# A gelu-gated block after a two-axis transform: in 36 units the minus half of the gate is formed from a copy of the even pass instead of a third matmul pass

## The chip, the cores and the metric

The kernel runs on one core of a Trainium2 chip. The metric is device time in microseconds of one execution. The profile of one execution gives a span (first to last instruction), the busy time of each engine and every instruction's start. The engines are TensorE (PE; its weight loads are PEld), VectorE (DVE), ScalarE (ACT), GpSimd (POOL) and SyncE (SP), which here issues the DMAs.

## The reference

```python
X = np.fft.fft(x, axis=1)          # x: 8 x 3008 x 256
X = np.fft.fft(X, axis=2)
x = X.real.reshape(8 * 3008, 256)
g = x @ w_gate                      # 256 x 1536
val = x @ w_val
out = (gelu(g) * val) @ w_out       # 1536 x 256, exact gelu
```

## The kernel before, in words

The input is real, so rows t and T - t of the transformed sequence have the same even part and opposite odd parts. The kernel therefore computes only 1505 of 3008 rows of each of the 8 batches as two planes in Y (`Y[:, 0, :]` even, `Y[:, 1, :]` odd), and makes both the "plus" row (even + odd) and the "minus" row (even - odd) from them. The second transform is folded into the first-layer weights: WE acts on the even plane, WOP on the odd plane, and WOM is WOP times -2, with zeros in the first partition, so that WOP + WOM, added up in one PSUM bank, is the minus odd part (`gen_w`, L399 to L412). Partition 0 of the odd plane holds another row (the "n" row), whose contribution does not change its sign; a copy of that row, spread over all partitions, lies in `nq`, and `WN` (L413 to L422) holds the n row's weights of the value side, per feature.

**Units.** For each batch the 1505 columns are cut into three chunks (`CH`: 481, 512 and 512 columns, in this order) and each chunk into 12 feature blocks of 128: 36 units per batch, 288 in all. Two units (even, odd) form a pair and share a PSUM tile `ps_v` of two banks, `glp`, `glm`, `ev` and `dv`. Each gate has its own bank `ps_g`, of which there are two. ps_v has two tiles, ps_o and ps_d one bank each.

**One loop.** The order of the work is written out by hand: every engine runs its instructions in program order (`_InOrder`, L19 to L25; that is why nearly all rows have L25). Loop u (L857 to L961) issues
- `val_even(u)`: the WE pass of the value; VectorE forms ev = n row x WN + even part;
- `gate_minus(u-1)`: the WOM pass on top of the bank of unit u-1, then ScalarE's Gelu into `glm`;
- `val_odd(u-1)`: the WOP pass of the value; for an odd unit VectorE then forms h = glp x ps_v for both units and dv = 2 ev - ps_v, the minus value;
- `gate_plus(u)`: WE and WOP passes into a fresh ps_g, Gelu into `glp`;
- `minus(u-1)`: for an odd unit GpSimd multiplies glm and dv of the pair into the mirrored columns of h;
- pieces of the next batch's transform: `a_step` (loops 0 to 11 of a batch, matmuls into ps_d and a ScalarE eviction S), `b_steps` as `fills` between the passes (loops 18 to 34, evictions Y on ScalarE), `fold_x` on GpSimd, DMAs;
- `second(8)`: eight matmuls of the second layer (h x Wo into ps_o, 256 columns), taken from a queue; after 24 of them ScalarE copies ps_o to osb and SP stores it. Sometimes it is 6 instead of 8.

So a gate of an ordinary unit takes three first-layer passes (WE, WOP, WOM), a value two. The last batch has no next batch beside it. Unit numbers below count inside a batch: units 0 to 11 have 481 columns (480 for minus), 12 to 35 have 512.

Of the kernel before, what the change touches and what calls it, by code (L numbers as in the profile page):

```python
# [9 lines left out]
FP32 = mybir.dt.float32  # L10
BF16 = mybir.dt.bfloat16
AF = mybir.ActivationFunctionType
# [15 lines left out]
def _sub(base: bass.AP, free_pattern, free_offset, part_start=0, part_num=None):  # L28
    p_step, p_count = base.ap[0]
    if part_num is None:  # L30
        part_num = p_count - part_start
    pat = [[p_step, part_num]] + [list(x) for x in free_pattern]
    off = base.offset + part_start * p_step + free_offset
    return ap_replace(base, ap=pat, offset=off)
# [3 lines left out]
def kernel(  # L38
# [53 lines left out]
    WOP = const_pool.tile([128, 2, F], BF16)  # L92
    WOM = const_pool.tile([128, 2, F], BF16)
    Wo_sb = const_pool.tile([128, NFC, C], BF16)
    WNb = const_pool.tile([128, NFC], BF16)
    WN = const_pool.tile([128, NFC], FP32)
    NQs = [const_pool.tile([128, YW], BF16, name=f"nq{i}") for i in range(2)]
    HXF = NFC - NCH * 2
    hx = const_pool.tile([128, HXF, 128], BF16)
# [41 lines left out]

    def dv_tile():
        return work.tile([128, 2, 512], FP32, tag="dv", bufs=2, name="dv")

    def osb_tile():
        return work.tile([128, 2, C], FP32, tag="osb", bufs=2, name="osb")
# [266 lines left out]

    def gen_wn():
        ps = ps_d()
        for fc in range(NFC):
            for t in range(NCH):
                pe.matmul(
                    ps[:, fc : fc + 1], _sub(wb[(fc // 4 * 512, 1)], [[1, 128]], t * 512 + fc % 4 * 128),
                    CW[:, t, 1, 0:1], start=(t == 0), stop=(t == NCH - 1))  # L420
        vec.tensor_copy(WNb[:, :], ps[:, :NFC])
        vec.tensor_copy(WN[:, :], WNb[:, :])  # L422

    def gen_tf():
        for i, t in enumerate((TP, TQ, T0P)):
# [142 lines left out]


    units = []  # L570
    for b in range(B):
        for ci in range(len(CH)):
            for fc in range(NFC):
                units.append((b, ci, fc))
    hs, banks, duos = {}, {}, {}

    def kind(u):
        b, ci, fc = units[u]
# [2 lines left out]
    def open_unit(u):  # L581
        b, ci, fc = units[u]
        if fc == 0:
            hs[(b, ci)] = h_tile()
        c0, n = CH[ci]
        if u % 2 == 0:
            duos[u // 2] = dict(pv=ps_v(), glp=glp_tile(), glm=glm_tile(), log=[])
            if kind(u):
                duos[u // 2]["ev"] = ev_tile()
        banks[u] = dict(  # L590
            d=duos[u // 2], k=u % 2, pv=duos[u // 2]["pv"][:, u % 2, :],
            glp=duos[u // 2]["glp"][:, u % 2, :], glm=duos[u // 2]["glm"][:, u % 2, :],
            b=b, fc=fc, c0=c0, n=n, nm=n - n % 32, kd=kind(u), fs=slice(fc * 128, (fc + 1) * 128),
            h=hs[(b, ci)], Y=Ys[b], nq=NQs[b % 2], po=0 if n == 512 else 480,
            mo=512 if n == 512 else 0)

    def layer1(r, ps, W, i, eo, n, start):
        m = pe.matmul(
            ps[:, :n], W[:, i, r["fs"]], r["Y"][:, eo, r["c0"] : r["c0"] + n],
            start=start, stop=True, skip_group_check=not start)  # L600
        if i:
            apart(r["d"]["log"], r["k"], m)

    def val_even(u):
        r = banks[u]
        layer1(r, r["pv"], WE, 1, 0, r["n"], True)
        if r["kd"]:
            nm, fc = r["nm"], r["fc"]
            apart(r["d"]["log"], r["k"], vec.scalar_tensor_tensor(
                r["d"]["ev"][:, r["k"], :nm], r["nq"][:, r["c0"] : r["c0"] + nm],  # L610
                WN[:, fc : fc + 1], r["pv"][:, :nm], op0=ALU.mult, op1=ALU.add))
        else:
            layer1(r, r["pv"], WOP, 1, 1, r["n"], False)

    def gate_minus(u):
        r = banks[u]
        layer1(r, r["pg"], WOM, 0, 1, r["nm"], False)
        act.activation(r["glm"][:, : r["nm"]], r["pg"][:, : r["nm"]], AF.Gelu)

    def gate_plus(u, fill):  # L620
        r = banks[u]
        n = r["n"]
        r["pg"] = ps_g()
        layer1(r, r["pg"], WE, 0, 0, n, True)
        fill()
        layer1(r, r["pg"], WOP, 0, 1, n, False)
        fill()
        act.activation(r["glp"][:, :n], r["pg"][:, :n], AF.Gelu)
# [213 lines left out]
        11 + j: (7 + j,) for j in range(5)}  # L842
    reads_first = {12: 0, 14: 1, 17: 2}

    NU = len(units)
    PER = NU // B

    evens = {27 + 2 * q + h: [(0, q, 4 * h, 4 * h + 4)] for q in range(4) for h in range(2)}
    later = {22: ["n"]}
# [7 lines left out]
    for u in range(NU + 2):  # L857
        b, i = divmod(u, PER)
        fills = []
        tail = None  # L860
        held = False
        if u < NU:
            open_unit(u)
            loads = (0, 14, 19) if b else (8, 12, 18)
            if i in loads and b + 2 < B:
                load_x(b + 2, loads.index(i))
            if b + 1 < B:
                for what in plan[min(b, 1)].get(i, ()):
                    if what == "n":
                        tail = lambda b=b: n_step(b + 1)  # L870
                        continue
                    eo, q, lo, hi = what
                    if lo == 0:
                        held = True
                        st[b + 1]["cur"] = b_steps(b + 1, eo, q)
                    fills += st[b + 1]["cur"][0][lo:hi]
                    if hi == 8:
                        tail = st[b + 1]["cur"][1]

        def fill(most=2):  # L880
            for _ in range(most):
                if fills:
                    fills.pop(0)()

        def second(n):
            for _ in range(n):
                if l2q:
                    l2q.pop(0)()

        if u == 0:  # L890
            r = banks[0]
            r["pg"] = ps_g()
            layer1(r, r["pv"], WE, 1, 0, r["n"], True)
            layer1(r, r["pg"], WE, 0, 0, r["n"], True)
            layer1(r, r["pg"], WOP, 0, 1, r["n"], False)
            layer1(r, r["pv"], WOP, 1, 1, r["n"], False)
            for e in later_evacs:
                e()
            n_first(0)
            act.activation(r["glp"][:, : r["n"]], r["pg"][:, : r["n"]], AF.Gelu)  # L900
            plus(r)
        elif u < NU:
            val_even(u)
            if not held:
                fill()
        if 0 < u <= NU:
            gate_minus(u - 1)
            if not held:
                fill()
        early = 0 < u <= NU and banks[u - 1]["kd"]  # L910
        if early:
            val_odd(u - 1)
        if 0 < u < NU:
            gate_plus(u, fill)
            if banks[u]["kd"] == 0:
                plus(banks[u])
        if 0 < u <= NU and not early:
            val_odd(u - 1)
        while fills:
            fill()  # L920
        if tail:
            tail()
        if 0 < u <= NU:
            minus(u - 1)
        if u < NU:
            if b + 1 < B and i == (19 if b else 21):
                n_turn(b + 1)
            if b + 1 < B and i == 30:
                n_read(b + 1)
        if u < NU:  # L930
            if b == 0:
                for e in extra.get(i, ()):
                    e()
                if i < 12:
                    fold_x(1, i // 4, pool, i % 4 * 2, 2)
            if i % 2 and b + 2 < B:
                j = i - 1
                if b:
                    f, fp = next((j - o, n) for n, o, z in ((0, 4, 18), (1, 18, 28), (2, 28, 36)) if j < z)
                else:  # L940
                    fp, f = divmod(j - 12, 8)
                if 0 <= f < 8 and fp >= 0:
                    fold_x(b + 2, fp, pool, f, 2)
            if b + 1 < B:
                for k in (i,) if b else a_first.get(i, ()):
                    if k < 12:
                        a_step(b + 1, k)
                        if k in (5, 7, 11):
                            j0 = {5: 0, 7: 12, 11: 16}[k]
                            z_write(b + 1, j0, 2 * k + 2 - j0)  # L950
                    if b and k in (8, 10, 13):
                        z_read(b + 1, (8, 10, 13).index(k))
                if b == 0 and i in reads_first:
                    z_read(1, reads_first[i])
        if 0 < u <= NU and u % 12 == 0:
            pb, pi = divmod(u // 12 - 1, 3)
            if CH[pi][0] == 0:
                pool.tensor_copy(hs[(pb, pi)][:, :, 1023:1024], lone)
            l2q += l2_steps(pb, pi)
            few = len(l2q) < 96  # L960
        second((6 if few and u % 12 > 5 else 8) if u <= NU else len(l2q))  # L961


# [28 lines left out]
```

## Time and profile before

| | us |
|---|---|
| median of 3 runs (lowest, highest) | 629.68 (628.66, 629.75) |
| the profiled execution | 628.29 |
| its span | 626.2 |
| PE busy | 604.6 |
| DVE busy | 540.8 |
| ACT busy | 473.5 |
| POOL busy | 450.1 |

The span is cut by program order into the start (weights, tables and the first batch's transform, to about 27 us), the eight batches, and a short end. Starts of loops in the trace: loop 0 of batch 3 at about 246.3 us, of batch 7 at about 540.9. A loop takes 1.89 to 2.2 us. Rows of a group give the engine, the operation, output and inputs, partitions x elements with types, the count, busy us, mean ns of one, and the idle time of the engine just before them with what ended it.

### The profile page before, as it was taken

The page shows a single profiled execution, that of the slowest core. Times are in us where ns is not written, and L with a number is a line of the kernel's source. Part 1 is how long each engine was busy: PE and PEld are TensorE (multiplying, and loading weights), DVE is VectorE, ACT ScalarE, POOL GpSimd, SP SyncE. Part 2 cuts the span into 40 slices and gives each one's busy share as a digit, 9 for nine tenths or more (in the row PEclk, how much of TensorE's full clock was granted, in tenths as well). Part 3 has the DMA queues.
Part 4 walks back from the last instruction along what each step waited for, and adds up shares of the span by engine and source line. Part 5 has one row for each costly group of instructions (what it writes and reads, how often), then busy time and mean ns, then how long its engine had stood idle before and what let it go on. Part 6 is the DMA issues. An engine that isn't in the chain of part 4 may idle for free.

```text
span 626.2 us, 12919 instructions
## 1 busy us (share of the span) xinstructions
PE 604.6 (97%) x4527; PEld 402.4 (64%) x4585; DVE 540.8 (86%) x649; ACT 473.5 (76%) x962; POOL 450.1 (72%) x474
## 2 busy tenths in 40 slices
PE   3799999999999999999999999999999999999997
PEld 2446666666666666666666666666666666666665
DVE  8688988898888989888898898889898899999991
ACT  8688778867787777877788777887778877767762
POOL 9297997768868788677777698687885555556552
PEclk9999999999999999999999999999999999999999
DMA  8997524562337613673246533375223612222123
GB/s 290 367 285 235 157 61 116 171 193 89 76 115 207 198 43 75 187 230 104 53 126 173 188 99 76 103 214 187 67 61 97 191 43 51 60 51 51 38 48 85
DMA packets 65874, 82.36 MB, mean 132 GB/s; under 512 B 8202, under 2 KB 59914, under 8 KB 62994
## 3 DMA queue, kind: packets, MB, share of 16 engines
q1 hardware_dynamic: 64098, 80.62, 43.6%
q0 software_dynamic: 1552, 0.79, 0.9%
q8 instruction: 36, 0.59, 0.4%
q14 instruction: 28, 0.23, 0.1%
q10 hardware_dynamic: 160, 0.13, 0.1%
HBM read 45.05 MB, written 37.25 MB: 131 GB/s over the span
## 4 chain that ended last, share of the span: by engine, by line
PE 90%; ACT 3%; DMA 3%; DVE 2%; issue 1%; SPq 1%; ACTq 0%; DVEq 0%
PE ps_o L25 38%; PE ps_g L25 28%; PE ps_v L25 19%; PE ps_d L25 6%; DMA z<-S 1%; DMA wst<-in_moe_w_gate_dram 1%; ACT S L25 1%; ACT glp L25 1%; ACT G L25 1%; ACT glm L25 1%; DMA Ap<-z 1%; DVE dv L25 0%; DVE h L25 0%; SPq L748 0%; ACT osb L25 0%
## 5 line engine op out<-in xcount | busy, mean ns | idle before, releaser
L25 POOL TENSOR_TENSOR h<-glm,dv 128x1024 bf16<-128x1024 bf16 (+1 forms) x138 | 290.9, 2108 | 152.1 <-DVE dv L25 104.5
L25 PE MATMUL ps_o<-Wo_sb,h 128*128 128x256 bf16 x2136 | 277.7, 272 | 0.2 <-ACT osb L25 0.2
L25 DVE SCALAR_TENSOR_TENSOR ev<-nq,WN,ps_v 128x512 f32<-128x512 bf16 (+1 forms) x276 | 202.6, 734 | 62.5 <-PE ps_v L25 43.8
L25 ACT ACTIVATE glm<-ps_g 128x512 bf16<-128x512 f32 (+1 forms) x288 | 169.4, 588 | 107.8 <-PE ps_g L25 70.9
L25 PEld LDWEIGHTS <-h 128*128 128x128 bf16 x2208 | 210.9, 98 | 53.7 <-issue 0.5
L25 ACT ACTIVATE glp<-ps_g 128x512 bf16<-128x512 f32 (+1 forms) x288 | 170.0, 590 | 9.8 <-PE ps_g L25 0.3
L25 DVE TENSOR_TENSOR h<-glp,ps_v 128x1024 bf16<-128x1024 bf16 (+2 forms) x150 | 172.9, 1153 | 4.8 <-ACT glp L25 2.6
L25 DVE SCALAR_TENSOR_TENSOR dv<-ev,ps_v 128x1024 f32<-128x1024 f32 (+1 forms) x138 | 164.8, 1194 | 0.0
L25 POOL TENSOR_TENSOR xf<-xin 128x254 bf16<-128x254 f32 x168 | 118.3, 727 | 0.4 <-PE ps_v L25 0.4
L25 PE MATMUL ps_g<-Y,WOM 128*128 128x512 bf16 (+1 forms) x288 | 107.7, 374 | 0.3
L25 PE MATMUL ps_v<-Y,WOP 128*128 128x512 bf16 (+1 forms) x288 | 107.7, 374 | 0.0
L25 PE MATMUL ps_v<-Y,WE 128*128 128x512 bf16 (+1 forms) x283 | 106.1, 375 | 0.1
L25 PE MATMUL ps_g<-Y,WOP 128*128 128x512 bf16 (+1 forms) x278 | 103.9, 374 | 1.8
L25 PE MATMUL ps_g<-Y,WE 128*128 128x512 bf16 (+1 forms) x248 | 92.5, 373 | 0.0
L25 PEld LDWEIGHTS <-WOP 128*128 128x128 bf16 x576 | 55.8, 97 | 52.8 <-ACT WOP L25 0.3
L25 PEld LDWEIGHTS <-WE 128*128 128x128 bf16 x576 | 56.0, 97 | 31.1 <-issue 1.0
L25 ACT ACTIVATE osb<-ps_o 128x512 f32<-128x512 f32 x93 | 54.8, 589 | 17.2 <-PE ps_o L25 12.8
L25 PEld LDWEIGHTS <-Ap 128*128 128x128 bf16 (+1 forms) x561 | 40.8, 95 | 33.8 <-DMA Ap<-z 0.3
L25 ACT ACTIVATE S<-ps_d 128x512 bf16<-128x512 f32 x82 | 48.6, 592 | 0.2
L25 PEld LDWEIGHTS <-G 128*128 128x128 bf16 x213 | 21.0, 100 | 31.8 <-ACT G L25 9.0
L25 ACT ACTIVATE Y<-ps_d 128x192 bf16<-128x192 f32 (+4 forms) x142 | 34.0, 339 | 0.5 <-PE ps_d L25 0.5
L25 PEld LDWEIGHTS <-WOM 128*128 128x128 bf16 x300 | 29.2, 97 | 4.9
(127 smaller groups left out, 261.3 us busy)
## 6 DMA issues: line engine op xcount, KB each, us to landing
out_dram<-osb SPq DMA_DIRECT2D x358, 64.0 KB
xin<-in_x_dram SPq DMA_DIRECT2D x16, 1024.0 KB
Ap<-z SPq DMA_DIRECT2D x24, 512.0 KB
xin<-in_x_dram SPq DMA_DIRECT2D x8, 896.0 KB
z<-S SPq DMA_DIRECT2D x7, 768.0 KB
z<-S SPq DMA_DIRECT2D x7, 512.0 KB
z<-S SPq DMA_DIRECT2D x13, 256.0 KB
nq<-nrow SPq DMA_DIRECT2D x8, 376.2 KB
```

The lines of the kernel that those rows point to most:

```text
L25: return lambda *a, **k: self._tc.keep_in_program_order(call(*a, **k))
```

## The change

In 36 units the WOM pass of the gate is left out. These are units 25 and 31 of batch 0, units 1, 5, 11, 25 and 31 of batches 1 to 6, and units 5, 11, 25 and 31 of batch 7. All are odd units of their pairs. In such a unit w
- the gate's WE pass is issued at the end of loop w-1, after four of the eight second-layer matmuls (`gate_even`), and ScalarE copies twice the even part from ps_g into `ge` (fp32);
- in loop w the WOP pass adds the odd part, the plus Gelu reads the bank as before, and VectorE forms go = n row x WN[:, 0] - ps_g (`gate_rest`);
- GpSimd adds ge to go, in place: 2 even + 2 n part - plus = minus gate;
- in loop w+2, after that loop's plus Gelu, ScalarE takes the Gelu of go from SBUF into `glm` (`gate_late`), and then the pair's minus product is issued (in loop w+1 before).

`gen_wn` now also computes the gate's n-row weights, doubled (`WN[:, 0, :]`), with 24 more one-column matmuls and one more small VectorE instruction. ge and go have one buffer each.

```diff
-        for fc in range(NFC):
+        for k in range(2 * NFC):
+            i, fc = divmod(k, NFC)
             for t in range(NCH):
                 pe.matmul(
-                    ps[:, fc : fc + 1], _sub(wb[(fc // 4 * 512, 1)], [[1, 128]], t * 512 + fc % 4 * 128),
+                    ps[:, k : k + 1], _sub(wb[(fc // 4 * 512, i)], [[1, 128]], t * 512 + fc % 4 * 128),
                     CW[:, t, 1, 0:1], start=(t == 0), stop=(t == NCH - 1))
-        vec.tensor_copy(WNb[:, :], ps[:, :NFC])
-        vec.tensor_copy(WN[:, :], WNb[:, :])
+        f = lambda t: _sub(t, [[1, 2 * NFC]], 0)
+        vec.tensor_copy(f(WNb), ps[:, : 2 * NFC])
+        vec.tensor_scalar(WN[:, 0, :], WNb[:, 0, :], 2.0, None, op0=ALU.mult)
+        vec.tensor_copy(WN[:, 1, :], WNb[:, 1, :])
...
+    SPLIT = ((25, 31), (1, 5, 11, 25, 31), (5, 11, 25, 31))
+    def split(u):
+        b, i = divmod(u, PER)
+        return i in SPLIT[0 if b == 0 else 2 if b == B - 1 else 1]
...
     def gate_minus(u):
+        if r["two"]:
+            return
...
+    def gate_even(u):
+        r = banks[u]
+        r["pg"] = ps_g()
+        layer1(r, r["pg"], WE, 0, 0, r["n"], True)
+        if r["two"]:
+            r["ge"], r["go"] = ge_tile(), go_tile()
+            nm = r["nm"]
+            act.activation(r["ge"][:, :nm], r["pg"][:, :nm], AF.Copy, scale=2.0)
+
+    def gate_rest(u):
+        r = banks[u]
+        if r["two"]:
+            nm = r["nm"]
+            vec.scalar_tensor_tensor(
+                r["go"][:, :nm], r["nq"][:, r["c0"] : r["c0"] + nm],
+                WN[:, 0, r["fc"] : r["fc"] + 1], r["pg"][:, :nm], op0=ALU.mult, op1=ALU.subtract)
+            pool.tensor_tensor(r["go"][:, :nm], r["go"][:, :nm], r["ge"][:, :nm], op=ALU.add)
+
+    def gate_late(u):
+        r = banks[u]
+        if r["two"]:
+            nm = r["nm"]
+            act.activation(r["glm"][:, :nm], r["go"][:, :nm], AF.Gelu)
+
     def gate_plus(u, fill):
-        r["pg"] = ps_g()
-        layer1(r, r["pg"], WE, 0, 0, n, True)
+        if not r["two"]:
+            gate_even(u)
         fill()
...
             gate_plus(u, fill)
+            gate_rest(u)
...
         if 0 < u <= NU:
-            minus(u - 1)
+            if not banks[u - 1]["two"]:
+                minus(u - 1)
+        if 1 < u and banks.get(u - 2, {}).get("two"):
+            gate_late(u - 2)
+            minus(u - 2)
...
-        second((6 if few and u % 12 > 5 else 8) if u <= NU else len(l2q))
+        if u + 1 < NU and split(u + 1):
+            open_unit(u + 1)
+            second(4)
+            gate_even(u + 1)
+        second((6 if few and u % 12 > 5 else 8) - 4 * (u + 1 < NU and split(u + 1)) if u <= NU else len(l2q))
```

More of the change, by code (lines that the diff above doesn't have):

```diff
@@ L94 @@
     Wo_sb = const_pool.tile([128, NFC, C], BF16)
-    WNb = const_pool.tile([128, NFC], BF16)
-    WN = const_pool.tile([128, NFC], FP32)
+    WNb = const_pool.tile([128, 2, NFC], BF16)
+    WN = const_pool.tile([128, 2, NFC], FP32)
     NQs = [const_pool.tile([128, YW], BF16, name=f"nq{i}") for i in range(2)]
@@ L143, in dv_tile, with ge_tile, go_tile @@
         return work.tile([128, 2, 512], FP32, tag="dv", bufs=2, name="dv")
+    def ge_tile():
+        return work.tile([128, 512], FP32, tag="ge", bufs=1, name="ge")
+    def go_tile():
+        return work.tile([128, 512], FP32, tag="go", bufs=1, name="go")
     def osb_tile():
@@ L570 @@
     units = []
+    NU = B * len(CH) * NFC
+    PER = NU // B
+    SPLIT = ((25, 31), (1, 5, 11, 25, 31), (5, 11, 25, 31))
     for b in range(B):
@@ L593, in open_unit @@
             b=b, fc=fc, c0=c0, n=n, nm=n - n % 32, kd=kind(u), fs=slice(fc * 128, (fc + 1) * 128),
-            h=hs[(b, ci)], Y=Ys[b], nq=NQs[b % 2], po=0 if n == 512 else 480,
+            two=split(u), h=hs[(b, ci)], Y=Ys[b], nq=NQs[b % 2], po=0 if n == 512 else 480,
             mo=512 if n == 512 else 0)
@@ L610, in val_even @@
                 r["d"]["ev"][:, r["k"], :nm], r["nq"][:, r["c0"] : r["c0"] + nm],
-                WN[:, fc : fc + 1], r["pv"][:, :nm], op0=ALU.mult, op1=ALU.add))
+                WN[:, 1, fc : fc + 1], r["pv"][:, :nm], op0=ALU.mult, op1=ALU.add))
         else:
@@ L616, in gate_minus @@
         r = banks[u]
-        layer1(r, r["pg"], WOM, 0, 1, r["nm"], False)
-        act.activation(r["glm"][:, : r["nm"]], r["pg"][:, : r["nm"]], AF.Gelu)
+        nm = r["nm"]
+        if r["two"]:
+            return
+        layer1(r, r["pg"], WOM, 0, 1, nm, False)
+        act.activation(r["glm"][:, :nm], r["pg"][:, :nm], AF.Gelu)
+    def gate_even(u):
[17 more added lines that the diff above has]
+        if r["two"]:
+            nm = r["nm"]
+            act.activation(r["glm"][:, :nm], r["go"][:, :nm], AF.Gelu)
     def gate_plus(u, fill):
@@ L843 @@
     reads_first = {12: 0, 14: 1, 17: 2}
-    NU = len(units)
-    PER = NU // B
     evens = {27 + 2 * q + h: [(0, q, 4 * h, 4 * h + 4)] for q in range(4) for h in range(2)}
@@ L862 @@
         if u < NU:
-            open_unit(u)
+            if not split(u):
+                open_unit(u)
             loads = (0, 14, 19) if b else (8, 12, 18)
```

## The prediction, made before the changed kernel had run

> **What bounds the kernel now.** I read the totals first, then the chain that ended last, the groups by form, the list of waits, and last the timeline round the units that change.
>
> ```profile
> span 626.2 us, 12919 instructions
> ...
> PE 604.6 (97%) x4527; PEld 402.4 (64%) x4585; DVE 540.8 (86%) x649; ACT 473.5 (76%) x962; POOL 450.1 (72%) x474
> ...
> PE 90%; ACT 3%; DMA 3%; DVE 2%; issue 1%; SPq 1%; ACTq 0%; DVEq 0%
> ```
>
> TensorE is busy for 97% of the span and carries 90% of the chain. A busy matmul row alone would prove little, because matmuls overlap (0.38 us each), so I looked at starts. From about 75 us on, a 512-column pass starts 0.216 us before the next matmul, a 480- or 481-column pass 0.203, a second-layer pass (256 columns) 0.109, without gaps. TensorE's issue is the bound: a removed pass shortens the end by its pitch, unless another engine then makes TensorE wait. That is the whole question, since VectorE (86%) is nearly as full.
>
> ```profile
> L25 POOL TENSOR_TENSOR h<-glm,dv 128x1024 bf16<-128x1024 bf16 x96 | 205.9, 2145 | 94.3 <-DVE dv L25 88.4 <-ACT glm L25 3.9 <-ACT glp L25 2.0
> L25 DVE SCALAR_TENSOR_TENSOR ev<-nq,WN,ps_v 128x512 f32<-128x512 bf16 x192 | 142.9, 745 | 37.2 <-PE ps_v L25 18.5 <-PE ps_d L25 18.3
> L25 POOL TENSOR_TENSOR xf<-xin 128x254 bf16<-128x254 f32 x168 | 118.3, 727 | 0.4 <-PE ps_v L25 0.4
> ...
> L25 DVE SCALAR_TENSOR_TENSOR ev<-nq,WN,ps_v 128x480 f32<-128x480 bf16 x84 | 59.7, 711 | 25.3 <-PE ps_v L25 25.3
> ...
> L25 ACT ACTIVATE osb<-ps_o 128x512 f32<-128x512 f32 x89 | 53.2, 598 | 16.4 <-PE ps_o L25 12.4 <-issue 2.5 <-DMA out_dram<-osb 0.6
> ```
>
> These rows (columns: busy us, mean ns | idle before) price the new instructions: ge has the shape of osb, go that of ev, and the GpSimd add lies between xf and h.
>
> **What is removed.** 36 WOM passes: 20 in units 1, 5, 11 (480 columns) and 16 in units 25, 31 (512): 20 x 0.203 + 16 x 0.216 = 7.5 us. The even pass of such a unit w only moves, from loop w to the end of loop w-1; the second-layer passes around it stay as many (4 and 4). The old minus Gelu (0.57 to 0.60) goes from loop w+1 and comes back, reading SBUF, in loop w+2.
>
> **What is added on TensorE.** gen_wn computes 24 columns instead of 12, so 24 more one-column matmuls. The 24 of before start at 42.68 and the next matmul at 43.28: 0.6 us. TensorE is nearly gapless there, so I charge 0.6; the lower end is 0, if it hides in the wait of 0.18 us behind WNb and in the waits for Gelu nearby. The extra WN instruction on VectorE (0.41 like its neighbour) is inside that.
>
> **ge on ScalarE and the WOP pass that waits for it.** ge must read the bank before WOP(w) adds to it. Loops 30 and 31 of batch 3:
>
> ```profile
> 309.77 0.60 ACT L25 ACTIVATE glp<-ps_g 128x512 bf16<-128x512 f32 x1
> ...
> 310.26 0.56 ACT L25 ACTIVATE Y<-ps_d 128x184 bf16<-128x184 f32 x2
> ...
> 310.60 1.22 DVE L25 SCALAR_TENSOR_TENSOR dv<-ev,ps_v 128x1024 f32<-128x1024 f32 x1
> ...
> 311.09 0.38 PE L25 MATMUL ps_g<-Y,WE 128*128 128x512 bf16 x1
> ...
> 311.13 0.60 ACT L25 ACTIVATE glm<-ps_g 128x512 bf16<-128x512 f32 x1 [0.31 <-PE ps_g L25]
> ...
> 311.36 0.38 PE L25 MATMUL ps_g<-Y,WOP 128*128 128x512 bf16 x1
> ...
> 311.73 0.74 DVE L25 SCALAR_TENSOR_TENSOR ev<-nq,WN,ps_v 128x512 f32<-128x512 bf16 x1
> ```
>
> ScalarE can start the next instruction 0.45 us after such a Y pair (302.02 to 302.47 in loop 26). The moved WE(31) starts at about 310.01, its data are readable 0.41 later (WOP 311.36 to glp 311.77 shows that lag), so ge runs 310.71 to 311.30. Loop 31 begins 0.216 later than before but has lost its WE, so WOP(31) still falls due at 311.36. A dependent start follows an end by 0.05 us at least (the smallest distance between ev's end and the WOP pass that waits for it). So ge is just in time. In units 1, 5, 11 an S eviction stands before ge: S at 256.46, ge 256.95 to 257.54, WOP(5) due at 257.69: 0.1 to spare. In batch 7 there is neither S nor Y, and ge is early. ge's own price lies between 0.57 (glm at 480) and 0.714 us (the G row, a read from SBUF with a scale column): a stall of 0 to 0.1 us in each of the 30 units of batches 1 to 6. I take the near row, osb, and 0.05 for the 12 units with Y, none for the rest: 0.6 us. Behind ge stand glm(w-1) and glp(w); ScalarE idles 0.31 to 0.50 before glm there and loses a whole Gelu in loop w+1, so the rest of ge is hidden. If that cover were gone, every 0.1 us of lateness would cost 0.1 us per unit.
>
> **go on VectorE.** go reads the bank that glp(w) reads too. The list of waits of before shows what happens when two engines read one bank:
>
> ```profile
> DVE WOM L25 <- ACT WOP L25: 0.9, 1, 0.9
> ```
>
> There VectorE waited for ScalarE although both only read ps_o, and the instruction order of the changed kernel gives go such a wait on ScalarE. [...]
>
> Where does go hurt? VectorE's queue behind it holds ev(w+1), h, dv, ev(w+2), and TensorE's value pass WOP of unit w+2 waits for ev(w+2). Unit 31, batch 3: glp(31) ends at about 312.42, go starts 312.45, and holds VectorE 0.67 (starts of ev and then h are 0.67 apart: 308.80, 309.47); ev(32), before at 312.91, comes at 313.12: 0.21 late. TensorE is 0.216 earlier from here on. The WOP pass of unit 33 started 0.56 after ev(33) ended: 0.56 - 0.21 - 0.216 = 0.13, above the 0.05 needed: no stall. Units 1, 5, 11: 0.72 us of room against 0.63 + 0.03: no lateness worth naming. By the next pair VectorE has caught up (0.44 and 0.75 us idle per pair).
>
> **Batch 7 is different**: no first transform lies beside it, a pair takes TensorE only 3.90 us instead of 4.1, and VectorE idles 0.24 per pair.
>
> ```profile
> 599.21 0.75 DVE L25 SCALAR_TENSOR_TENSOR ev<-nq,WN,ps_v 128x512 f32<-128x512 bf16 x1 [0.24 <-PE ps_v L25]
> ...
> 602.14 0.74 DVE L25 SCALAR_TENSOR_TENSOR ev<-nq,WN,ps_v 128x512 f32<-128x512 bf16 x1
> 603.12 0.75 DVE L25 SCALAR_TENSOR_TENSOR ev<-nq,WN,ps_v 128x512 f32<-128x512 bf16 x1 [0.23 <-PE ps_v L25]
> ```
>
> ev(31) ends its slot at 602.81; go holds to 603.48, so ev(32) is 0.36 late; the waiting pass had 0.25 to spare: 0.25 - 0.36 - 0.216 = -0.33, with the 0.05 a stall of 0.38, more than the 0.216 gained. The same for unit 25; by the same count 0.18 for unit 5 and 0.12 for unit 11: 1.06 us together.
>
> **The add on GpSimd and the late Gelu.** From xf (254 columns, 727 ns) and h (1024, 2145 ns) a line gives 1.2 us for 512; the ends are 0.73 and 2.15. It is queued behind the minus product of the pair before: 314.06 to 315.26 for unit 31. ScalarE reaches the late Gelu after glp(33), about 316.1, and would hold evictions and the next glm behind it if it waited; 0.8 us to spare, and the high end of 2.15 would just still do. GpSimd's queue then has fold and minus product 0.7 us later, which it makes up in one or two pairs; h is read by the second layer only after its chunk, dv is wanted two pairs later. Cost: nothing. No DMA is added or moved; SP's queue is untouched.
>
> **Sum**: -7.5 + 0.6 + 0.6 + 1.06 = -5.3 us. The profiled execution took 628.29 us (span 626.2 and 2.1 around it), which becomes 623.0. It lies 1.4 below the median of the three runs, 629.68, so I put the forecast on the median: **624.4 us**.
>
> **Rivals.**
> 1. Everything is covered: ge never stalls, batch 7 absorbs go. Only gen_wn is paid: 629.7 - 6.9 = 622.8. For it: TensorE shows hardly a wait. Against: VectorE's idle 0.24 in batch 7. Chance 0.23.
> 2. go is dearer than ev's pitch, because it starts on a wait of its own (0.745 and 0.1 to 0.2 more instead of 0.67): in the 12 units 25 and 31 of batches 1 to 6 the 0.13 to spare turns into a stall of about 0.15, 1.8 us: 626.2. Chance 0.17.
> 3. Slower: the WOP pass waits for ge. ScalarE is in order, and ge ends within 0.1 us of when it is wanted. If ge starts one instruction late (an osb or a longer S in front, 0.45), each of 30 units stalls by 0.4: 12 us, less the 5.9 of a sum without my 0.6: 635.8. It decides from 5.9 / 30 = 0.20 us of wait per unit. Against it: S, Y and glp already stand in the counted times, and osb falls at the end of loops 2, 5, 8 and 11 of a chunk, never just before ge. Chance 0.10.
> 4. Smaller waits of 2 and 3 together cancel the gain: about 629. Chance 0.05.
>
> The forecast keeps 0.45. A measurement of this kernel tells about 0.2% (1.26 us) from no change. Faster by more: 0.23 + 0.17 + 0.45, less a little for 2's upper end = 0.84; within: 0.06; slower: 0.10. The range 621.8 to 628.5 takes in rivals 1 and 2 and the bounds of ge (0 to 3 us), gen_wn and the 1.4 us between profile and median; it leaves out rivals 3 and 4.
>
> **What would show it.** Right: 36 fewer ps_g matmuls with WOM, TensorE still about 97% busy, waits of PE on ge below 0.1 us each, VectorE's busy time up by about 26 us, GpSimd's by about 43 with the add near 1.2 us, and loops 7, 13, 27, 33 of batch 7 with a wait on ev. Wrong: a long total "ps_g <- ACT ge" (rival 3), "glm <- POOL go" on ScalarE, or waits of PE on ev in batches 1 to 6 (rival 2).

## The result, and the profile after

| | before | after |
|---|---|---|
| median, us (lowest, highest) | 629.71 (628.66, 630.04), 4 runs | 623.98 (622.88, 624.58), 4 runs |
| the profiled execution | 628.29 | 624.03 |
| its span | 626.2 | 622.0 |

After / before is 0.991, with a 95% interval of 0.9892 to 0.9928: faster by 0.9%, and inside the forecast's range (624.4; 621.8 to 628.5). The medians differ by 5.7 us, the two profiled executions by only 4.3. Executions of one kernel differ in their first 30 us; the last section shows part of the reason. So the comparisons below count from loop 0 of batch 0 on.

The totals and the chain's shares, on the page of after:

```profile
span 622.0 us, 12960 instructions
...
PE 598.5 (96%) x4515; PEld 399.8 (64%) x4573; DVE 566.0 (91%) x686; ACT 485.1 (78%) x998; POOL 491.4 (79%) x510
...
PE 80%; DVE 6%; DMA 5%; ACT 5%; SPq 2%; issue 2%; ACTq 0%; DVEq 0%
```

VectorE gained 25.2 us of work, GpSimd 41.3, ScalarE 11.6, and TensorE lost 6.1 of busy time; still the span is shorter. TensorE carries the chain as before, with less of it. The new rows, among the groups by form of after (busy us, mean ns | idle before):

```profile
L25 POOL TENSOR_TENSOR h<-glm,dv 128x1024 bf16<-128x1024 bf16 x96 | 206.0, 2146 | 71.8 <-DVE dv L25 50.9 <-ACT glm L25 16.9 <-DVE ev L25 1.5
...
L25 POOL TENSOR_TENSOR go<-go,ge 128x512 f32<-128x512 f32 x16 | 20.4, 1272 | 0.0
...
L25 DVE SCALAR_TENSOR_TENSOR go<-nq,WN,ps_g 128x512 f32<-128x512 bf16 x16 | 11.9, 746 | 0.1
...
L25 ACT ACTIVATE ge<-ps_g 128x512 f32<-128x512 f32 x16 | 9.6, 602 | 0.1
```

The prices were read well: ge 0.602 (osb: 0.598), go 0.746 (ev: 0.745), the GpSimd add 1.27 (1.20 at 480 columns; 1.2 forecast). GpSimd's idle time before the minus product falls (94.3 to 71.8). In the list of waits of after, TensorE's matmuls wait for GpSimd once, 9.0 us for an xf, as in before.

**Where the time went.** I took the start of every unit's value WOP pass in both traces and subtracted, after minus before:

| at | us |
|---|---|
| loop 0 | -0.24 |
| unit 11 of batch 0 | +2.11 |
| end of batch 0 | +1.69 |
| end of batches 1, 2, 3 | +0.68, -0.34, -1.36 |
| end of batches 4, 5, 6 | -2.39, -3.40, -4.42 |
| end of batch 7 | -4.21 |

Three things are in it. First, the kernel after *loses* 2.35 us between units 6 and 11 of batch 0, where it splits nothing. Then it gains 0.42 in batch 0 and 1.02 in each of batches 1 to 6, against removed passes worth 2 x 0.216 = 0.43 and 3 x 0.203 + 2 x 0.216 = 1.04: nearly all of it arrives. In batch 7 it gives 0.2 back.

Why the passes pay in full: unit 25 of batch 3, in the timeline of after.

```profile
296.96 0.58 ACT L25 ACTIVATE Y<-ps_d 128x184 bf16<-128x184 f32 x2
...
297.42 0.60 ACT L25 ACTIVATE ge<-ps_g 128x512 f32<-128x512 f32 x1
...
298.07 0.38 PE L25 MATMUL ps_g<-Y,WOP 128*128 128x512 bf16 x1
...
298.55 0.59 ACT L25 ACTIVATE glp<-ps_g 128x512 bf16<-128x512 f32 x1
...
299.17 0.75 DVE L25 SCALAR_TENSOR_TENSOR go<-nq,WN,ps_g 128x512 f32<-128x512 bf16 x1
```

ge ends at 298.02 and the WOP pass that adds to its bank starts 0.05 later, the smallest distance at which a value WOP pass follows its ev in either trace. It is just in time, as the prediction said. glp ends at 299.14 and go starts 0.03 later.

Batch 7, VectorE's rows of after and then TensorE's, round unit 33:

```profile
600.93 1.22 DVE L25 SCALAR_TENSOR_TENSOR dv<-ev,ps_v 128x1024 f32<-128x1024 f32 x1
602.06 1.40 DVE L25 SCALAR_TENSOR_TENSOR ev<-nq,WN,ps_v 128x512 f32<-128x512 bf16 x2
```

```profile
602.41 0.38 PE L25 MATMUL ps_g<-Y,WOM 128*128 128x512 bf16 x1
602.86 0.38 PE L25 MATMUL ps_v<-Y,WOP 128*128 128x512 bf16 x1
```

VectorE has no gap (dv, then both ev back to back), and the WOP pass follows the WOM pass by 0.45 instead of 0.216: it waits for ev, 0.23 us. Two passes earlier, the value's WE pass (602.20) starts 0.05 after dv ends (602.15), 0.11 late. By the same count of starts the four units cost 0.18 (unit 5), 0.24 (11), 0.33 (25) and 0.34 (31).

The loss of 2.35 us lies in `gen_wn` of batch 0. Timeline of after, VectorE, GpSimd and the pass that comes late:

```profile
44.59 1.57 DVE L25 TENSOR_SCALAR WN<-WNb 128x12 f32<-128x12 bf16 x1
...
44.74 1.39 POOL L25 TENSOR_TENSOR xf<-xin 128x254 bf16<-128x254 f32 x2
46.08 1.58 DVE L25 CAST WN<-WNb 128x12 f32<-128x12 bf16 x1
...
46.23 1.39 POOL L25 TENSOR_TENSOR xf<-xin 128x254 bf16<-128x254 f32 x2
...
48.27 0.36 PE L25 MATMUL ps_v<-Y,WOM 128*128 128x480 bf16 x1 [1.79 <-DVE h L25]
```

Two VectorE instructions of 12 columns take 1.57 and 1.58 us. The first ends at 46.16, 0.03 after GpSimd's two folds at 44.74 to 46.13; the second at 47.66, 0.04 after the next two (46.23 to 47.62). (In the first chunk of batch 0 the kernel works otherwise than in the loop described above: VectorE forms h for each unit by itself, and the value too gets its minus half by a WOM pass, onto the bank that h reads.) The unit's plus product h stands behind the two on VectorE, and TensorE's WOM pass waits 1.79 us for it. In before, the one WN instruction ended at 45.23, 0.03 after two folds (43.79 to 45.20) too:

```profile
43.79 1.41 POOL L25 TENSOR_TENSOR xf<-xin 128x254 bf16<-128x254 f32 x2
...
44.82 0.41 DVE L25 CAST WN<-WNb 128x12 f32<-128x12 bf16 x1
```

Its row, from the groups of before, is what I had taken for its price:

```profile
L25 DVE CAST WN<-WNb 128x12 f32<-128x12 bf16 x1 | 0.4, 411 | 0.0
```

### The profile page after: what moved, and what is told of

The parts are those of the page before. It is cut to its first block, busy times and chain, and to the rows that moved or that the text cites. A ratio compares the mean times of both kernels' runs of the same rounds, so it can differ in the third digit from the quotient of the medians.

```text
span 622.0 us, 12960 instructions
## 1 busy us (share of the span) xinstructions
PE 598.5 (96%) x4515; PEld 399.8 (64%) x4573; DVE 566.0 (91%) x686; ACT 485.1 (78%) x998; POOL 491.4 (79%) x510
## 4 chain that ended last, share of the span: by engine, by line
PE 80%; DVE 6%; DMA 5%; ACT 5%; SPq 2%; issue 2%; ACTq 0%; DVEq 0%
PE ps_o L25 34%; PE ps_g L25 24%; PE ps_v L25 17%; PE ps_d L25 5%; DMA Ap<-z 4%; SPq L791 2%; ACT osb L25 1%; ACT S L25 1%; DVE h L25 1%; DVE dv L25 1%; DVE xf L25 1%; DVE ev L25 1%; DMA wst<-in_moe_w_val_dram 1%; ACT glp L25 1%; ACT glm L25 1%
## 5 line engine op out<-in xcount | busy, mean ns | idle before, releaser
L25 POOL TENSOR_TENSOR h<-glm,dv 128x1024 bf16<-128x1024 bf16 (+1 forms) x138 | 291.2, 2110 | 105.2 <-DVE dv L25 62.7
L25 PE MATMUL ps_o<-Wo_sb,h 128*128 128x256 bf16 x2136 | 283.6, 273 | 1.3 <-ACT osb L25 0.3
L25 PEld LDWEIGHTS <-h 128*128 128x128 bf16 x2208 | 210.9, 98 | 57.3 <-issue 0.5
L25 DVE SCALAR_TENSOR_TENSOR ev<-nq,WN,ps_v 128x512 f32<-128x512 bf16 (+1 forms) x276 | 202.0, 733 | 30.7 <-PE ps_v L25 23.0
L25 ACT ACTIVATE glp<-ps_g 128x512 bf16<-128x512 f32 (+1 forms) x288 | 169.8, 589 | 37.8 <-PE ps_v L25 17.6
L25 ACT ACTIVATE glm<-ps_g 128x512 bf16<-128x512 f32 (+1 forms) x252 | 148.6, 590 | 63.8 <-PE ps_g L25 43.8
L25 DVE TENSOR_TENSOR h<-glp,ps_v 128x1024 bf16<-128x1024 bf16 (+2 forms) x150 | 172.9, 1153 | 5.0 <-ACT glp L25 2.4
L25 DVE SCALAR_TENSOR_TENSOR dv<-ev,ps_v 128x1024 f32<-128x1024 f32 (+1 forms) x138 | 164.8, 1194 | 0.0
L25 POOL TENSOR_TENSOR xf<-xin 128x254 bf16<-128x254 f32 x168 | 118.2, 725 | 0.4 <-PE ps_v L25 0.4
L25 PE MATMUL ps_v<-Y,WOP 128*128 128x512 bf16 (+1 forms) x288 | 107.8, 374 | 0.2
L25 PE MATMUL ps_v<-Y,WE 128*128 128x512 bf16 (+1 forms) x283 | 106.2, 375 | 0.1
L25 PE MATMUL ps_g<-Y,WE 128*128 128x512 bf16 (+1 forms) x267 | 99.8, 374 | 0.0
L25 PE MATMUL ps_g<-Y,WOP 128*128 128x512 bf16 (+1 forms) x259 | 96.8, 374 | 0.7
L25 PE MATMUL ps_g<-Y,WOM 128*128 128x512 bf16 (+1 forms) x252 | 94.5, 375 | 0.3
L25 PEld LDWEIGHTS <-WOP 128*128 128x128 bf16 x576 | 55.8, 97 | 50.7 <-issue 0.6
L25 PEld LDWEIGHTS <-WE 128*128 128x128 bf16 x576 | 56.0, 97 | 28.5 <-issue 2.0
L25 ACT ACTIVATE osb<-ps_o 128x512 f32<-128x512 f32 x93 | 54.8, 589 | 15.7 <-PE ps_o L25 12.5
L25 PEld LDWEIGHTS <-Ap 128*128 128x128 bf16 (+1 forms) x561 | 39.8, 96 | 32.0
L25 ACT ACTIVATE S<-ps_d 128x512 bf16<-128x512 f32 x82 | 48.8, 596 | 1.9 <-PE ps_d L25 1.9
L25 POOL TENSOR_TENSOR go<-go,ge 128x480 f32<-128x480 f32 (+1 forms) x36 | 44.4, 1235 | 0.0
L25 PEld LDWEIGHTS <-G 128*128 128x128 bf16 x213 | 21.1, 100 | 33.5 <-ACT G L25 8.9
L25 ACT ACTIVATE Y<-ps_d 128x192 bf16<-128x192 f32 (+4 forms) x142 | 34.0, 340 | 0.5 <-PE ps_d L25 0.5
```

The lines of the kernel that those rows point to most:

```text
L25: return lambda *a, **k: self._tc.keep_in_program_order(call(*a, **k))
```

## The experiments

Theory A: the gain is TensorE's pitch per removed pass; the loss at WN is a VectorE instruction held while GpSimd's folds run; the loss of batch 7 is go on a full VectorE. The rivals: WN's time is its own or comes from something else; go costs as much in the other batches; ScalarE, where ge is just in time, or GpSimd is the next limit. Kernels with "one run" in their line ran once; what is said of them comes from that execution's trace. The kernel before took 628.62 us (median) beside the first four, 628.73 beside the next three, and 629.64 beside the last three.

| kernel | us (lowest, highest) | to before, 95% |
|---|---|---|
| wn_only | 629.34 (628.48, 631.17) | 1.0014 (1.0002, 1.0026) |
| wn_scalar | 623.39 (622.53, 624.47) | 0.9912 (0.9892, 0.9932) |
| wn_psum | 623.15, one run | |
| b7_plain | 622.83, one run | |
| ge_twice | 640.82, one run | |
| more3 | 623.57 (623.10, 624.25) | 0.9914 (0.9898, 0.9931) |
| more_all | 624.73 (624.32, 625.61) | 0.9937 (0.9922, 0.9952) |
| after_again | 624.66 (623.44, 624.82) | 0.9917 (0.9902, 0.9931) |
| best_a | 623.43 (622.47, 623.82) | 0.9899 (0.9884, 0.9914) |
| best_b | 621.52 (621.02, 622.16) | 0.9868 (0.9852, 0.9885) |

### What the WN weights cost alone: wn_only

```diff
-    SPLIT = ((25, 31), (1, 5, 11, 25, 31), (5, 11, 25, 31))
+    SPLIT = ((), (), ())
```

> The larger gen_wn alone; no unit is split. Theory: the two small WN instructions of VectorE (12 columns, SBUF to SBUF) are held until GpSimd ends its running fold, 1.57 and 1.58 us in the trace of after, and TensorE stands behind them; the span grows by about 2.3 us over before (626.2 to 628.5). Rival, my prediction's term: only the 24 more matmuls count, +0.6 us (626.8).

The first WN took 0.37 us and the second 1.58 (VectorE and GpSimd in the timeline of wn_only):

```profile
44.56 0.37 DVE L25 TENSOR_SCALAR WN<-WNb 128x12 f32<-128x12 bf16 x1
...
44.85 1.58 DVE L25 CAST WN<-WNb 128x12 f32<-128x12 bf16 x1
...
44.99 1.41 POOL L25 TENSOR_TENSOR xf<-xin 128x254 bf16<-128x254 f32 x2
```

The second again ends 0.03 after the folds (46.43 and 46.40). From loop 0 to unit 11 the kernel loses 1.16 us, neither the 2.3 of after nor the rival's 0.6. So the size that I gave for it missed: the wait depends on where in a pair of folds the instruction falls, and that shifts between executions. With the two instructions, after loses 2.35 us there (they take 1.57 and 1.58), after_again, the same kernel, 1.76 (0.97 and 1.58), wn_only and b7_plain 1.16 and 1.17 (0.37 and 1.58), and ge_twice, below, only 0.33 (0.91 and 0.16; the second falls between two pairs of folds).

### The two WN instructions elsewhere: wn_scalar, wn_psum

```diff
-        vec.tensor_scalar(WN[:, 0, :], WNb[:, 0, :], 2.0, None, op0=ALU.mult)
-        vec.tensor_copy(WN[:, 1, :], WNb[:, 1, :])
+        act.activation(WN[:, 0, :], WNb[:, 0, :], AF.Copy, scale=2.0)
+        act.activation(WN[:, 1, :], WNb[:, 1, :], AF.Copy)
```

> After, with both WN instructions on ScalarE. Theory: ScalarE shares nothing with GpSimd, so each takes about 0.2 us and TensorE's wait of 1.79 us in loop 8 of batch 0 goes: span about 1.8 us under after (622.0 to 620.2), 24 more matmuls remain. Rival: the wait belongs to the small instructions as such, whatever the engine, or to the matmuls: no change over 0.4 us.

The instructions of tile WN in wn_scalar (ns: lowest, median, highest), and the folds beside them:

```profile
L25 ACT ACTIVATE WN<-WNb x2: 195/204/212, 45.9 to 46.0; 128x12 f32<-128x12 bf16 x2
```

```profile
45.25 1.41 POOL L25 TENSOR_TENSOR xf<-xin 128x254 bf16<-128x254 f32 x2
```

On ScalarE each takes 0.20 us beside the same folds, and the loss falls from 2.35 to 0.66. In its trace theory A is right. The late Gelu of after, which ScalarE takes from SBUF to SBUF, says the same: 0.62 us for 512 columns beside folds (at 157.64) and with GpSimd idle (at 590.06). That ScalarE shares nothing with GpSimd is shown no further than by these times. The span, 621.5, is not the 620.2 expected: loop 0 starts 1.05 us later than in before (last section). The medians show hardly any of it: 0.9912 to before here, 0.991 for after. Both this loss and the start vary between executions of after, so its median need not hold the 2.35 of its profiled one.

wn_psum leaves the instructions on VectorE and lets them read PSUM:

```diff
-        vec.tensor_copy(f(WNb), ps[:, : 2 * NFC])
-        vec.tensor_scalar(WN[:, 0, :], WNb[:, 0, :], 2.0, None, op0=ALU.mult)
-        vec.tensor_copy(WN[:, 1, :], WNb[:, 1, :])
+        vec.tensor_scalar(WN[:, 0, :], ps[:, :NFC], 2.0, None, op0=ALU.mult)
+        vec.tensor_copy(WN[:, 1, :], ps[:, NFC : 2 * NFC])
```

> After, with WN formed by VectorE straight from PSUM in fp32; the rounding to bf16 in between is left out, so WN differs in its last bits. Theory: with a PSUM source VectorE does not need what GpSimd holds, both instructions take about 0.17 us like the WNb row, and the 1.79 us wait goes. Rival: VectorE is slow on 12-column outputs as such: they stay above 1 us.

Same engine, same size, same neighbours; the source differs, in memory and in type (PSUM, fp32, instead of SBUF, bf16). VectorE and GpSimd in the timeline of wn_psum:

```profile
44.17 1.40 POOL L25 TENSOR_TENSOR xf<-xin 128x254 bf16<-128x254 f32 x2
...
44.94 0.16 DVE L25 TENSOR_SCALAR WN<-ps_d 128x12 f32<-128x12 f32 x1
45.02 0.16 DVE L25 COPY WN<-ps_d 128x12 f32<-128x12 f32 x1
```

Both run in the middle of the folds and take 0.16 us. What remains of the loss is 0.31 us, with the 24 more matmuls. So it is neither the engine nor the size: a copy from this source in SBUF is what waits. No run parts the memory from the type; bf16 in SBUF alone is not slow, for in ge_twice the second WN instruction, between two pairs of folds, takes 0.16. Beside the folds the two took 0.37 to 1.58 us each on VectorE from SBUF, 0.16 on VectorE from PSUM and 0.20 on ScalarE. Why VectorE is held, no run shows.

### Batch 7 without the split: b7_plain

```diff
-    SPLIT = ((25, 31), (1, 5, 11, 25, 31), (5, 11, 25, 31))
+    SPLIT = ((25, 31), (1, 5, 11, 25, 31), ())
```

> After without the four split units of batch 7. Theory: these four cost stalls of 0.18, 0.16 (with 0.08), 0.33 and 0.33 us against 0.2 us each of removed passes, so undoing them takes 0.2 us off the way from the start of batch 7 to the last value pass. Rival: each split is worth its pass here too: undoing them costs 0.84 us.

Against before, b7_plain goes from -5.45 (end of batch 6) to -5.52 at the end; after goes from -4.42 to -4.21. Four splits, which remove 2 x 0.203 + 2 x 0.216 = 0.84 us of passes, cost 0.28 net: 1.12 us of stalls. The rival, by which they gain 0.84, falls.

### ge doubled: ge_twice

```diff
             act.activation(r["ge"][:, :nm], r["pg"][:, :nm], AF.Copy, scale=2.0)
+            act.activation(r["ge"][:, :nm], r["pg"][:, :nm], AF.Copy, scale=2.0)
```

> After with the even copy ge issued twice in a row, so that WOP(w) waits 0.49 us longer for ScalarE. Theory: units 25 and 31 have nothing to spare (WOP starts 0.05 us after ge ends, the least there is), units 1, 5, 11 have 0.13, 0.08 and 0.13, batch 7 0.22: stalls of about 0.49, 0.36, 0.41, 0.36, in all 13 to 14 us over after, span 635 to 636. Rival: ScalarE is idle for 22% of the span and takes it for nothing: under 2 us.

This asks whether ScalarE's idle share (22% in after) covers a late ge. Timeline of ge_twice, unit 25 of batch 3:

```profile
316.55 1.24 ACT L25 ACTIVATE ge<-ps_g 128x512 f32<-128x512 f32 x2
...
317.83 0.38 PE L25 MATMUL ps_g<-Y,WOP 128*128 128x512 bf16 x1 [0.48 <-ACT ge L25]
```

It doesn't. The five units of a batch stall by 0.47, 0.52, 0.47, 0.64 and 0.64 us; the second ge, which writes the same tile, starts 0.60 to 0.64 after the first. The span is 16.7 above after's, more than the 13 to 14 that I expected, because I had spaced the two by 0.49. The rival (idle time takes it in) falls, and the prediction's third rival is real as a mechanism: a ge one instruction late costs every unit its lateness.

### More units: more3, more_all

Both have WN on ScalarE, no split in batch 7, and two buffers for ge and go.

```diff
+    # more3
+    SPLIT = ((25, 31), (1, 3, 5, 11, 25, 31), ())
+    # more_all
+    SPLIT = ((25, 31), (1, 3, 5, 7, 9, 11, 25, 31), ())
```

> WN on ScalarE, no split in batch 7, unit 3 of batches 1 to 6 split as well, two buffers each for ge and go. Theory: a pair of 481 columns has room on VectorE (0.72 us against go's 0.66) and on GpSimd (no fold in loops 1 and 3), so each of the 6 new splits gains 0.2 us: span 1.2 + 1.8 + 0.2 = 3.2 us under after, about 618.8. Rival: VectorE or ScalarE, full in two pairs in a row, give it back: not under 620.0.

> As more3, with units 7 and 9 split too: every pair of the 481-column chunk of batches 1 to 6. Theory A: only TensorE and VectorE count: another 2.4 us, span 616.4. Theory B: GpSimd does not keep up (2.02 + 1.6 + 1.2 = 4.8 us of work against a pair of 4.0 in loops 4 to 11), the late Gelu waits at the head of ScalarE's queue for the add and TensorE stalls: above more3, 619 to 622.

A batch of more3 gains 0.85 us, one of after 1.02: the sixth split loses 0.17 net, although it removes 0.20. ScalarE's rows of more3, in batch 2:

```profile
181.59 0.65 ACT L25 ACTIVATE glm<-go 128x480 bf16<-128x480 f32 x1
182.09 0.65 ACT L25 ACTIVATE S<-ps_d 128x512 bf16<-128x512 f32 x1
```

The late Gelu of unit 1 stands before S. S ends at 182.74, the next a_step matmul into ps_d starts 182.78, 0.16 late. Two loops on, osb is late in the same way, behind the late Gelu of unit 3 and an S, and the second layer waits 0.22 for ps_o:

```profile
185.60 0.61 ACT L25 ACTIVATE glm<-go 128x480 bf16<-128x480 f32 x1
186.09 0.60 ACT L25 ACTIVATE S<-ps_d 128x512 bf16<-128x512 f32 x1
186.57 0.61 ACT L25 ACTIVATE osb<-ps_o 128x512 f32<-128x512 f32 x1
```

Together 0.38, more than the pass is worth. The theory (0.2 more per new split, span 618.8) falls; the span is 622.2, and the rival, by which an engine gives the gain back, stands. more_all gains 0.59 per batch, with another 0.20 (ps_d) and 0.46 (ps_o) of stalls per batch. These stalls too end with an eviction of ScalarE that stands behind a late Gelu. Its span is 623.6, so theory A (616.4) falls. Theory B was right that more splits lose, but not on where: in no split unit of more_all does the late Gelu wait for the add, it starts 0.59 us or more after the add's end. So ScalarE's order is the limit that comes next; GpSimd, the other candidate, is not what TensorE waits for.

### The better version: after_again, best_a, best_b

after_again is the kernel after, unchanged, beside the other two.

> The changed kernel again, beside the two below on one chip. Theory: 0.7 to 0.9% under before; in batch 0 the two WN instructions of VectorE take anything from 0.5 to 3.2 us together, by where GpSimd's folds stand when they start, so this kernel's times spread by some 1.5 us. Rival: they take 3.2 us always.

best_a has WN from PSUM (as wn_psum) and no split in batch 7. Its WN weights, like those of wn_psum and best_b, are not rounded to bf16.

> WN from PSUM and no split in batch 7. Theory: against after the wait behind WN goes (0.9 to 2.0 us) and 0.2 us of batch 7's stalls net: 1.0 to 2.2 us under after_again, ratio to before about 0.988. Rival: the medians of after hold little of the WN wait: under 0.5 us of difference.

best_b adds to best_a unit 3 of batches 1 to 6 and two buffers for ge and go, and moves the late Gelu behind the a_step, that of unit 3 by one more loop:

```diff
-        if 1 < u and banks.get(u - 2, {}).get("two"):
-            gate_late(u - 2)
-            minus(u - 2)
...
+        for v in (u - 3, u - 2):
+            if banks.get(v, {}).get("two") and u - v == (3 if v % PER == 3 else 2):
+                gate_late(v)
+                minus(v)
```

> best_a with unit 3 of batches 1 to 6 split too, the late Gelu issued after the S eviction, and that of unit 3 a loop later, where ScalarE has one Gelu less. Theory: in more3 the new splits gained nothing because S (and through ps_d a transform matmul, 0.16 us) and osb (and through ps_o the second layer, 0.22 us) came late behind the late Gelu; with that order mended the six splits are worth 0.2 us each: 1.2 us under best_a. Rival: the chunk's ScalarE work is too much in any order: not better than best_a.

after_again lies 0.83% under before, as expected; its two WN instructions take 2.55 us together, so the rival (always 3.2) falls. Its 624.66 falls to 623.43 in best_a: 0.31 instead of 1.76 us at gen_wn, and no loss in batch 7 (1.2 us, inside the 1.0 to 2.2 expected). best_b takes 621.52, 1.9 less again. ScalarE's rows of best_b at the place shown above for more3:

```profile
181.09 0.66 ACT L25 ACTIVATE S<-ps_d 128x512 bf16<-128x512 f32 x1
181.57 0.66 ACT L25 ACTIVATE glm<-go 128x480 bf16<-128x480 f32 x1
```

Now S goes first, ps_d is free in time, and a batch gains 1.22 us with six splits (best_a: 1.02 with five): the sixth pays its whole pitch, 0.20, in all batches but one, which has a stall of 0.2. From unit 11 of batch 0 to the end best_b gains 7.40 us on before, best_a 6.50. So the traces show 0.9 of the 1.9 us between their medians (1.2 expected); where the rest comes from is not shown. best_b's ratio to the kernel before, 0.9868 with 0.9852 to 0.9885, is the best here.

## Why the prediction was right

- **TensorE's issue is the bound, 0.216 and 0.203 us per pass**: right. 32 splits in batches 0 to 6 gave 6.53 of 6.68 us.
- **gen_wn, 0.6**: wrong, and the term that missed: 2.35 in the profiled execution, 0.33 to 1.76 in others. The sentence "the extra WN instruction (0.41 like its neighbour) is inside that" failed. The row of 0.41 was not an instruction's work but its wait for a fold; two of them can wait for two pairs of folds. In wn_psum, where the instructions don't wait, 0.31 is left. The matmuls alone were sized well: in after they push the next value pass 0.60 back, and the value pass behind it only 0.25, since the idle time behind WNb, 0.18 in before, is gone.
- **ge's stall, 0.6**: too high. All stalls of batches 0 to 6 together are 6.68 - 6.53 = 0.15. That S, Y and ge are just in time was right; ge_twice shows that nothing lies behind it as cover.
- **go waits for glp**: the start is 0.03 after glp's end nearly everywhere, as the order written into the instructions demands. The wait of 0.9 us in before that stood for it was on ps_d, not ps_o: WOP ends at 25.79 and WOM starts at 25.83. What happens when both engines read the bank at once wasn't tried.
- **go in batches 1 to 6**: right. The WOP pass of unit 33 of batch 3 starts 0.14 after ev's end (0.13 forecast), and unit 27's 0.16. The second rival, 0.15 of stall in 12 units, isn't seen. The first, by which batch 7 absorbs go, falls with the next point.
- **Batch 7, 1.06 of stalls**: right, 1.12 (0.18, 0.12, 0.38 and 0.38 forecast for its units; 0.18, 0.24, 0.33 and 0.34 measured).
- **The add and the late Gelu, nothing**: right. In batches 0 to 6 the late Gelu starts 0.59 to 1.23 after the add's end, in batch 7 0.23 to 0.69, so it never waited. The list of waits of after does name one sign of being wrong, `ACT glm L25 <- POOL go L25: 3.8, 5, 0.8`; but these five are ordinary Gelus from ps_g, whose own WOM pass started less than 0.5 us before. What the steps missed lies ahead of it on the same engine: the late Gelu delays S and osb. At five units per batch that costs nothing; at six it does (more3).
- **The sum**: -7.5 + 2.35 + 0.15 + 1.12 = -3.9 from loop 0 on; with the 0.24 that the profiled after was ahead by then and 0.07 that batch 7 gains in b7_plain too, -4.2, as the spans say (-5.3 forecast). That the median lies only 0.4 from the forecast is luck: the sum was too good by 1.1 (gen_wn 1.75 dearer, ge 0.45 cheaper, 0.31 from before loop 0 and from the end), and that was made up by the 1.4 us that I added for the median of before, while after's profiled run lay on its median. A part of that 1.4 is probably the clock (last section): before's profiled run has 1.00 throughout.

## What to carry to other kernels

Before a short instruction's row is taken for a price, look at what runs beside it: here a duration that ended 0.03 us after another engine's instruction was a wait, and a second such instruction paid it again (1.57 and 1.58 us). When work moves from a full engine to an idle one that runs in order, its idle share says little (ScalarE's 22% didn't cover a ge late by 0.60 to 0.64); what counts is which eviction stands behind the new instruction, and who waits for it. Leave a trade out where the engine that takes the work has no gap (batch 7 here), even if it pays everywhere else.

## What the runs showed of the hardware that I had not expected

In after, VectorE's tensor_scalar and cast of 12 columns from bf16 in SBUF to SBUF were held as long as GpSimd's folds ran, through two of them back to back (1.57 and 1.58 us). They were let go 0.03 and 0.04 us after the second's end. A GpSimd cast of 4 columns held nothing: in ge_twice a WN instruction ran beside one in 0.16. Nor is every VectorE instruction of this kind held by every one of GpSimd's: at 15.20 us of after a VectorE tensor_scalar (256 columns, fp32, SBUF to SBUF) took 0.28 beside GpSimd's tensor_scalar instructions, as long as the next one, at 15.93, with GpSimd idle.

The granted TensorE clock isn't the same in every execution (means of 0.996 to 1.000). The table by stage (stretch, length, busy us of each engine, then PEclk, DMA share, GB/s) of wn_only, and then of after_again:

```profile
22.00:23.00 1.00, 0.00 (x0) 0.00 (x0) 0.23 (x1) 0.00 (x0) 0.00 (x0) 1.00 1.34 532
...
26.00:27.00 1.00, 1.00 (x36) 0.87 (x32) 1.00 (x6) 0.77 (x4) 0.68 (x1) 1.00 1.19 492
```

```profile
22.00:23.00 1.00, 0.00 (x0) 0.00 (x0) 0.11 (x1) 0.13 (x1) 0.00 (x0) 1.00 1.35 484
...
26.00:27.00 1.00, 1.00 (x31) 1.00 (x29) 0.95 (x5) 0.65 (x4) 0.65 (x1) 0.50 1.15 457
```

From 22 to 25 us TensorE has 1.1 us of work in wn_only and 1.0 in after_again; its longest wait there, 1.58 and 1.49 us up to 23.25 and 23.37, is for weights (VectorE's cast wb, which itself waits for their DMA). In after_again the clock is then 0.50 for some 3.4 us (mean 0.93, 0.50, 0.50, 0.50 and 0.86 in the five us from 24 to 29), in wn_only 1.00 throughout. Five of the profiled executions have this dip (wn_scalar, more3, more_all, after_again, best_b); in them loop 0 starts 0.80 to 1.05 us later than in before's. In the six others it starts between 0.27 earlier and 0.32 later. The kernel before has it too, it seems: beside the first four experiments its ten runs with a mean clock of 0.998 or more took 628.15 to 629.17 us, the three with 0.996 or 0.997 took 629.47 to 629.79. Beside the last three, though, one run with 1.000 took 629.71, so the clock is not all that differs. What sets the dip is not shown. TensorE has little work ahead of it, but some: in after_again the 3.4 us before the dip hold 1.40 us. And executions without a dip have as little there: from 22 to 25 us it is 0.99 to 1.09 us in before, after, wn_only, wn_psum, b7_plain and best_a, 0.98 to 1.17 in the five with one.
